# Order of the first steps and of the gathers and gates between attention and experts, in an attention-to-experts kernel on one Trainium2 core

## The chip, the cores and the metric

The kernel runs on one core of one Trainium2 chip, so there is no other core to exchange data with. The core has five engines that run side by side, each with its own instruction stream, and wait for one another by semaphores: TensorE (PE, matrix products and transposes), VectorE (DVE), ScalarE (ACT), GpSimd (POOL) and SyncE (SP, which here only issues transfers). Data lies in SBUF; matrix products land in PSUM; transfers between the device's memory and SBUF are done by 16 DMA engines. The metric is the device time of one execution in microseconds (us), as the median over runs. Beside the timed runs there is one execution with the hardware profiler, from which the page and every start time below come; it took 531.48 us, of which 529.5 lie between the first and the last instruction.

## The reference

The input is q, k, v of shape (4, 8, 768, 64) in float32: four batches, eight heads, 768 positions. Stage one is attention with a Λ-shaped mask and a linear bias per head; stage two sends each of the 3072 resulting tokens to one of eight experts.

```python
scores = scale * np.matmul(q, k.transpose(0, 1, 3, 2))
is_global = pos[None, :] < int(n_global)            # the first 8 positions
is_local = (rel >= 0) & (rel < int(n_local))        # the last 96 positions
keep = is_global | is_local
dist = np.where(is_global & ~is_local, float(n_local), np.abs(rel))
scores = np.where(keep, scores - slopes * dist, -1e9)
a = softmax(scores)
x = (a @ v).transpose(0, 2, 1, 3).reshape(3072, 512)

logits = x @ w_gate                                 # 8 experts
expert_idx = np.argmax(logits, axis=1)
gate_w = softmax(logits)[arange, expert_idx]
for e in range(8):                                  # tokens of expert e
    y[e] = np.maximum(x[e] @ w1[e], 0.0) @ w2[e]    # 512 -> 1024 -> 512
return gate_w[:, None] * y
```

## The kernel before

**Attention (to 161 us).** Positions are cut into six blocks of 128. A query block sees its own and the previous key block and the eight global keys. Heads go in pairs, two heads of 64 side by side in 128 partitions; 4 batches times 4 pairs give 16 pairs, in the code `pr`. A pair is worked in three units of two blocks each, so there are 48 units, `units[n]`. For a unit, `scores(n)` makes the products of Q with K (L507), ACT takes the exponential (L513, tile `e`), and DVE multiplies by the bias weights `Wb` (L520 for a pair's first unit, L524 for the others). `attend(n)` multiplies by V (L542, tile `o`), two units behind the scores; `turn(n)` transposes the attention's results (L559, tile `px`, copied at L561) for the router.

The keys come in two forms. `kT` holds K transposed. `kA` is a shifted copy, in which the first 8 columns of each block are replaced by the eight global keys; `keys_at` makes it with two ACT copies (L426 for the rest of the block, L428 for the global ones). Likewise `va` is V with the global rows in it (`turn_v`, ACT copies L452 and L453). `Wb` for a pair of heads is made by `weights(j)` with two ACT exponentials (L486) of the distances `distb`, which `bias()` builds on DVE (L477 to L482).

From the second pair on, K and Q come in strips by SP's transfers (L409) and DVE transposes them (`turn_qk`, L461 and L462). The first pair is different: its K and Q are loaded whole (`load_first`, blocks 0 to 2 first, then 2 to 6) and turned by PE against an identity matrix (`turn_first`, L442), as a first lot of two blocks before the scores of unit 0 and a second lot of four blocks after them. A lot's K is copied out of PSUM by DVE (L443), its Q by ACT (L444), then ACT makes `kA`. `weights(0)` is called ahead of unit 0's scores.

**Between attention and experts (161 to 197 us).** Each finished batch is routed: `logits`, `spread`, `tables` and `spread_sum` count the tokens of each expert and give each its place. Expert 0's first 256 tokens are worked early, in 16 small pieces of PE work (`early_hidden`, L347, and `early_result`, L354), which `work(n)` takes off a list `fill`, so that PE has something to do while DVE, ACT and POOL do the routing of the last batch. `fetch_0(i)` gathers these tokens from the device's memory by POOL's indirect transfers into `xq_0`; `take(1)` gathers those of the next expert, its `xq_0` and `xq_s` pieces, back to back (L284), and the early outputs `y_0_0` and `y_0_1` are written out after that. `xq_0` and `xq_s` are filled with zeros once (L211 and L774), so that the rows that no token fills are defined. `gates_of` (L273 to L280) multiplies the gate weights into a sparse form `mg` on DVE, sums them by a product (`pg`, L279, a tile of the pool `ps_m`) and copies the result out on DVE (L280); it is called twice in a row, between two calls of `work`.

**Experts (from 197 us).** The eight experts follow in order of size, with capacities of 464 tokens down to 272; expert 0 has 208 left after its early 256. `hidden(p)` makes the 1024 hidden values in eight steps (L1065), each followed by ACT's relu (L1067); `result(p)` or `along_row` makes the 512 outputs (L1102 or L1119). `pace(n, after)` issues up to n waiting gathers on POOL behind a given instruction, so that they are spread over an expert's work. `sort` transposes gathered tokens on DVE (L295).

What sets the order: the engines' streams are written out by hand under a manual schedule, so every engine runs its instructions as the Python code issues them; the pools' buffer counts and the semaphores that the framework derives set the waits. `tc.add_manual_dep`, in `behind`, adds a wait on a named instruction.

Of the kernel before, what the change touches and what calls it, by code (L numbers as in the profile page):

```python
# [16 lines left out]
P = 128  # L17
# [12 lines left out]
def kernel(  # L30
# [76 lines left out]

    ones_in(vts[0])

# [5 lines left out]
    iota_c = consts.tile([P, 1], F32)  # L115
    iota(iota_c, [[0, 1]], 0, 1)

    warm = consts.tile([P, 1], F32)
    nc.vector.memset(warm, 0.0)
    nc.scalar.activation(warm, warm, AF.Exp)  # L120
    load_first(2, NB)
    ident = consts.tile([P, P], F32)
    make_identity(nc, ident)
    rank_e = consts.tile([P, E], F32)
# [147 lines left out]

    def gates_of(pool, ps, nm, ns, gs, to):  # L273

        mg = pool.tile([P, NS, TB], F32, tag="mw", name="mg" + nm, bufs=1)[:, 0:ns, :]
        nc.vector.tensor_tensor(out=mg, in0=gs.rearrange("p (s o) -> p s o", o=1).to_broadcast([P, ns, TB]),
                                in1=grp.rearrange("p (o g) -> p o g", o=1).to_broadcast([P, ns, TB]), op=ALU.mult)
        pg = ps.tile([P, NS * TB], F32, tag="m", name="pg" + nm)[:, 0:TB * ns]
        nc.tensor.matmul(pg, lhsT=sel, rhs=mg.rearrange("p s g -> p (s g)"), start=True, stop=True)  # L279
        nc.vector.tensor_copy(out=to, in_=pg)  # L280

# [17 lines left out]
    def plan(p):  # L299
        if p < E:  # L300
            r = ORDER[p] - 2
            xqs[p] = xq_s[p % 2]
            cols = rows_0[1][:, 2 * TB:] if p == 1 else rows_s[:, NQ * TB * r:NQ * TB * r + NQ * TB]
            for i in range(pieces_of(CAPS[ORDER[p]])):
                pending.append((xqs[p], cols, i))

# [9 lines left out]
    def take(p):  # L316
        plan(p)
        while pending:
            gather_one(*pending.pop(0))

# [21 lines left out]
    def hidden_0(ph, q, f0, nf):  # L342

        for f in range(nf):
            c0 = P * (f0 + f)
            for kc in range(KC):
                nc.tensor.matmul(ph[:, P * f:P * f + P], lhsT=w1_0[:, 0, kc, c0:c0 + P], rhs=xe_0[:, kc, P * q:P * q + P],  # L347
                                 start=(kc == 0), stop=(kc == KC - 1))
        nc.scalar.activation(hT_0[q][:, f0:f0 + nf, :], ph.rearrange("p (f s) -> p f s", f=nf), AF.Relu)

    def result_0(po, q, f0, nf, later=None):

        for fc in range(f0, f0 + nf):
            nc.tensor.matmul(po, lhsT=hT_0[q][:, fc, :], rhs=w2_0[:, 0, fc, :],  # L354
                             start=(fc == 0), stop=(fc == FC - 1))
        if f0 + nf == FC:
            scaled(f"y_0_{q}", P, po, gslot_0[0][:, q:q + 1], idx_0[0][:, q:q + 1], later)

    def distances(dist, kpos, loc):
# [16 lines left out]
    def banded_attention():  # L376
        with ExitStack() as actx:
# [46 lines left out]

            def keys_at(kT, kA, a0, a1):
                nc.scalar.copy(out=kA[:, a0:a1, GW:P],  # L426
                                      in_=kT[:, a0 * P:a1 * P].rearrange("p (c t) -> p c t", t=P)[:, :, GW:P])
                nc.scalar.copy(out=kA[:, a0:a1, 0:GW],  # L428
                                      in_=kT[:, 0:GW].rearrange("p (o t) -> p o t", o=1).to_broadcast([P, a1 - a0, GW]))

# [4 lines left out]

            def turn_first(c0, c1, pt):

                qT, kT, kA = pairs[0][0:3]
                w = P * (c1 - c0)
                for i, t in enumerate((k_first, q_first)):  # L440
                    for c in range(c0, c1):
                        nc.tensor.transpose(pt[:, i, P * (c - c0):P * (c - c0) + P], t[:, c, :, :].rearrange("p h d -> p (h d)"), ident)  # L442
                nc.vector.tensor_copy(out=kT[:, P * c0:P * c1], in_=pt[:, 0, 0:w])  # L443
                nc.scalar.copy(out=qT[:, P * c0:P * c1], in_=pt[:, 1, 0:w])  # L444
                keys_at(kT, kA, max(c0 - 1, 0), c1 - 1)

# [45 lines left out]
            def blocks(c):  # L492

                return [(0, True), (1, False), (1, True)] if c == 0 else [(0, False), (0, True), (1, False), (1, True)]

            def scores(n):
                b, j, c = units[n]
                qT, kT, kA = pairs[b * NJ + j][0:3]
                bl = blocks(c)
                w = P * len(bl)  # L500
                ps = ps_s.tile([P, 2, 512], F32, tag="s", name=f"s_{n}")
                for m, (t, own) in enumerate(bl):
                    i = 2 * c + t
                    for h in range(2):
                        r = slice(D * h, D * h + D)
                        lhsT = kT[r, P * i:P * i + P] if own else kA[r, i - 1, :]
                        nc.tensor.matmul(ps[:, h, P * m:P * m + P], lhsT=lhsT, rhs=qT[r, P * i:P * i + P],  # L507
                                         start=True, stop=True)
# [4 lines left out]
                nc.scalar.activation(e[:, :, 0:w], ps[:, :, 0:w], AF.Exp, scale=D ** -0.5)  # L513
                if n == 0:
                    turn_first(2, NB, ps_s.tile([P, 2, 512], F32, tag="s", name="first_1"))
                    turn_v(0)
                elif c == 1 and b == 0 and j + 1 < NJ:
                    weights(j + 1)
                if c == 0:
                    nc.vector.tensor_tensor(out=e[:, :, 0:w], in0=e[:, :, 0:w], in1=W[:, 2 * j:2 * j + 2, 0:w],  # L520
                                            op=ALU.mult)
                else:
                    eh = e.rearrange("p h (t c) -> p h t c", t=2)
                    nc.vector.tensor_tensor(  # L524
                        out=eh, in0=eh,
                        in1=W[:, 2 * j:2 * j + 2, P:3 * P].rearrange("p h (o c) -> p h o c", o=1).to_broadcast([P, 2, 2, 2 * P]),
                        op=ALU.mult)
                st[n] = e
# [134 lines left out]
            def early_hidden(z, f0):  # L663
                ph = ps_s.tile([P, 2, 512], F32, tag="s", name=f"ph_0_{z}_{f0}")
                hidden_0(ph[:, 0, 0:2 * P], z, f0, 2)

            def early_result(z, f0):
                if f0 == 0:
                    st["po"] = ps_o.tile([P, DM], F32, tag="o", name=f"po_0_{z}")
                result_0(st["po"], z, f0, 2, later)  # L670

# [72 lines left out]
            pair_tiles(0)  # L744
            turn_first(0, 2, ps_o.tile([P, 2, 2 * P], F32, tag="o", name="first_0"))
            bias()
            weights(0)
            nu = len(units)
# [5 lines left out]
            for n0 in range(0, nu, 2):  # L754
# [5 lines left out]
                for n in two:  # L760
# [238 lines left out]
    with tc.manual_schedule():  # L999
        banded_attention()  # L1000

        take(1)
        while later:
            later.pop(0)()


        r2 = recips.rearrange("p a b -> p (a b)")
# [15 lines left out]
        with ExitStack() as ectx:  # L1023
# [31 lines left out]
            def hidden(p, between=None):  # L1055
# [6 lines left out]
                for fc in range(FC):  # L1062
# [23 lines left out]
            def along_row(p, C, w2t, hT):  # L1086
# [127 lines left out]
```

## Time and profile before

| what | value |
| --- | --- |
| time, median of 3 runs | 519.71 us (519.63 to 520.02) |
| span of the profiled execution | 529.5 us |
| PE's first record, and its first scores | 4.67 us, 6.68 us |
| PE's first early piece of expert 0 after the last unit's product with V | 161.32 us |
| PE's first record of expert 0's rest | 196.97 us |
| PE's last record | 520.1 us |

The page of the profile gives, for each engine, the time in which it was busy; then the span in 40 slices of 13.2 us, where a digit is the busy share of a slice in tenths; then the transfers, and groups of instructions with the idle time ahead of them and what ended it. Tiles carry their names from the program, but where SBUF is used again under another name the trace shows the older one: `w_second` stands for several buffers of the attention stage. In a timeline a row is `start, duration, engine, line, operation, out<-in, shape, count`, with the idle time before it in brackets and what ended that. PE's rows overlap, since matrix products are pipelined; the distance of two starts is what one costs.

### The profile page before, as it was taken

Reading aid. Unit: us, or ns where it says so; the run is one execution under the profiler, and the core shown is the slowest. Engines: PE = TensorE matmul, PEld = TensorE weight load, DVE = VectorE, ACT = ScalarE, POOL = GpSimd, SP = SyncE. Lnnn points to the kernel's source line nnn. Section 1 sums busy time; section 2 is a strip of 40 time slices with the busy share of each in tenths; the row PEclk is TensorE's granted clock in tenths of the full one; section 3 lists DMA queues with packets and bytes.
Section 4 is the critical chain, followed back from the end, with each engine's and each line's share of the span. In section 5 each row is a group of like instructions: output and inputs, shape, how many; then the busy total and the mean of one; then the engine's idle time right before and its main releaser. Section 6 shows DMA issues by size and latency. Waiting matters only on the chain.

```text
span 529.5 us, 7971 instructions
## 1 busy us (share of the span) xinstructions
PE 503.4 (95%) x3108; PEld 348.2 (66%) x3108; DVE 181.3 (34%) x484; ACT 126.7 (24%) x227; POOL 138.5 (26%) x161
## 2 busy tenths in 40 slices
PE   4999999999999995999999999999999999999992
PEld 3989999999999744975455445545545846545540
DVE  5867897896975423010120030021011011020010
ACT  4766655654642100101001101100100201101100
POOL 5000000000042474243344145325114625310010
PEclk9999999999999998999999999999999999999997
DMA  9899999999919712490825456173372685110000
GB/s 152 149 166 162 236 171 163 232 182 168 315 49 248 230 46 65 100 277 27 182 71 190 100 130 202 42 171 104 130 153 86 198 188 190 39 41 17 1 35 27
DMA packets 145184, 71.95 MB, mean 136 GB/s; under 512 B 126672, under 2 KB 126678, under 8 KB 145136
## 3 DMA queue, kind: packets, MB, share of 16 engines
q1 hardware_dynamic: 137344, 58.16, 48.3%
q0 software_dynamic: 5264, 12.59, 7.8%
q10 hardware_dynamic: 2528, 0.59, 0.6%
q8 instruction: 26, 0.43, 0.4%
q14 instruction: 22, 0.18, 0.1%
HBM read 59.00 MB, written 12.75 MB: 135 GB/s over the span
## 4 chain that ended last, share of the span: by engine, by line
PE 82%; another core or an unknown queue 5%; SPq 5%; DVE 3%; DMA 2%; ACT 1%; issue 1%; POOL 0%; POOLq 0%; ACTq 0%; DVEq 0%
PE ph L1065 29%; PE po L1119 26%; PE o L542 11%; PE s L507 5%; SPq L409 4%; PE ph L347 2%; PE po L1102 2%; PE px L559 2%; PE pt L1128 1%; PE pq L573 1%; PE pi L632 1%; DMA vt<-in_v_dram 1%; DMA x_tok<-xr 1%; DMA k_first<-in_k_dram 1%
## 5 line engine op out<-in xcount | busy, mean ns | idle before, releaser
L1067 ACT ACTIVATE hT<-ph 128x416 f32<-128x416 f32 (+4 forms) x64 | 29.6, 467 | 289.2 <-PE ph L1065 179.1
L284 POOL DMA_INDIRECT xq_s<-x_tok,rows_s x72 | 72.6, 1009 | 67.9 <-ACT hT L1067 39.2
L1065 PE MATMUL ph<-xe,w_first 128*128 128x208 f32 (+3 forms) x256 | 79.3, 471 | 6.2 <-ACT hT L1067 4.5
L335 DVE TENSOR_SCALAR y<-po,gslot_s 128x512 f32<-128x512 f32 (+1 forms) x17 | 12.8, 751 | 201.5 <-PE po L1119 201.5
L1065 PE MATMUL ph<-xe,w_second 128*128 128x416 f32 (+3 forms) x256 | 79.4, 470 | 0.0
L1119 PE MATMUL po<-w_second,hT 128*128 128x512 f32 (+1 forms) x176 | 76.2, 592 | 0.0
L1065 PEld LDWEIGHTS ph<-xe,w_first 128*128 128x128 f32 x256 | 50.2, 200 | 34.4 <-issue 11.4
L1065 PEld LDWEIGHTS ph<-xe,w_second 128*128 128x128 f32 x256 | 48.3, 190 | 29.3 <-issue 10.4
L1119 PE MATMUL po<-w_first,hT 128*128 128x512 f32 (+1 forms) x144 | 62.3, 592 | 0.0
L1119 PEld LDWEIGHTS po<-w_second,hT 128*128 128x128 f32 (+1 forms) x176 | 33.2, 189 | 41.3 <-issue 40.7
L284 POOL DMA_INDIRECT xq<-x_tok,rows x15 | 16.0, 1068 | 162.1 <-DVE rows L271 143.4
L542 PE MATMUL o<-vt,e 128*128 128x128 f32 x288 | 53.2, 275 | 0.0
L327 POOL DMA_INDIRECT out_dram<-y,idx_s x17 | 17.2, 1011 | 124.7 <-DVE xe L295 71.7
L1119 PEld LDWEIGHTS po<-w_first,hT 128*128 128x128 f32 (+1 forms) x144 | 27.2, 189 | 34.0 <-issue 33.5
L542 PE MATMUL o<-va,e 128*128 128x128 f32 x240 | 46.6, 276 | 0.1
L542 PEld LDWEIGHTS o<-vt,e 128*128 128x128 f32 x288 | 42.4, 192 | 0.1
L507 PE MATMUL s<-qT,kT 64*128 64x128 f32 x384 | 38.6, 285 | 0.9 <-ACT qT L444 0.9
L513 ACT ACTIVATE e<-s 128x1024 f32<-128x1024 f32 (+1 forms) x36 | 33.2, 945 | 26.1 <-PE s L507 26.1
L507 PE MATMUL s<-qT,kA 64*128 64x128 f32 x320 | 34.3, 292 | 3.2 <-ACT kA L428 3.2
L542 PEld LDWEIGHTS o<-va,e 128*128 128x128 f32 x240 | 36.4, 192 | 0.4 <-issue 0.3
L507 PEld LDWEIGHTS s<-qT,kT 64*128 64x128 f32 x384 | 30.2, 196 | 2.2 <-ACT qT L444 1.3
L524 DVE TENSOR_TENSOR e<-e,Wb 128x1024 f32<-128x1024 f32 x24 | 28.7, 1210 | 7.6 <-ACT e L513 7.3
(189 smaller groups left out, 502.8 us busy)
## 6 DMA issues: line engine op xcount, KB each, us to landing
w_second<-in_moe_w_dram SPq DMA_DIRECT2D x16, 512.0 KB, 9.0
w_second<-in_moe_w_dram SPq DMA_DIRECT2D x4, 2048.0 KB
x_tok<-xr SPq DMA_DIRECT2D x24, 256.0 KB, 3.6
w_first<-in_moe_w_dram SPq DMA_DIRECT2D x12, 512.0 KB, 7.7
w_first<-in_moe_w_dram SPq DMA_DIRECT2D x3, 2048.0 KB
vt<-in_v_dram SPq DMA_DIRECT2D x31, 192.0 KB, 3.8
w_second<-in_q_dram SPq DMA_DIRECT2D x60, 96.0 KB, 3.3
w_second<-in_k_dram SPq DMA_DIRECT2D x60, 96.0 KB, 2.8
```

What stands on the lines that cost most here:

```text
L284: return nc.gpsimd.indirect_dma_start(out=xq[:, i, :], out_offset=None, in_=x_tok[0:NJ * top, :], in_offset=bass.IndirectOffsetOnAxis(ap=c ...
L327: p = nc.gpsimd.indirect_dma_start(out=to[:, :], out_offset=bass.IndirectOffsetOnAxis(ap=where, axis=0), in_=y[0:rows, :], in_offset=None, ...
L335: done = nc.vector.tensor_scalar(out=y[0:rows, :], in0=po[0:rows, :], scalar1=gs[0:rows, :], scalar2=None, op0=ALU.mult)
L347: nc.tensor.matmul(ph[:, P * f:P * f + P], lhsT=w1_0[:, 0, kc, c0:c0 + P], rhs=xe_0[:, kc, P * q:P * q + P], start=(kc == 0), stop=(kc == ...
L409: nc.sync.dma_start(t[p0:p0 + 32, :, :], src[b, 2 * j + h].rearrange("(c t) d -> t c d", t=32)[:, :, 32 * d:32 * d + 32])
L507: nc.tensor.matmul(ps[:, h, P * m:P * m + P], lhsT=lhsT, rhs=qT[r, P * i:P * i + P], start=True, stop=True)
L513: nc.scalar.activation(e[:, :, 0:w], ps[:, :, 0:w], AF.Exp, scale=D ** -0.5)
L524: nc.vector.tensor_tensor(out=eh, in0=eh, in1=W[:, 2 * j:2 * j + 2, P:3 * P].rearrange("p h (o c) -> p h o c", o=1).to_broadcast([P, 2, 2, ...
L542: nc.tensor.matmul(po[:, t, h, :], lhsT=pt[:, h, P * m:P * m + P], rhs=(vt if own else va)[:, c0:c0 + P], start=(m == mine[0][0]), stop=(m ...
L1065: nc.tensor.matmul(ph[:, 0:C], lhsT=w1t[:, 0, kc, P * fc:P * fc + P], rhs=xe[:, kc, 0:C], start=(kc == 0), stop=(kc == KC - 1))
L1067: done = nc.scalar.activation(hT[:, fc, 0:C], ph[:, 0:C], AF.Relu)
L1119: nc.tensor.matmul(po[0:rows, :], lhsT=hT[:, fc, P * q:P * q + rows], rhs=w2t[:, 0, fc, :], start=(fc == 0), stop=(fc == FC - 1))
```

## The change

The change has two halves. They have in common that work which isn't needed yet is taken out of the way of work that is.

At the start: POOL makes the identity matrix first and some constants later; the second half of the first pair's loads is issued on ACT before ACT loads its exponential table; the first pair is turned in three lots of two blocks, one before the scores of unit 0 and two behind them, with K and Q in separate PSUM tiles; the first pair's `kA` is copied by DVE in place of ACT; `weights(0)` is called after the second lot in place of ahead of unit 0; the zero fills of `xq_0` and `xq_s` wait for the exponentials of units 18, 24, 30 and 36.

At the passage to the experts: the gathers of expert 0's rest go through the list of waiting gathers, two at once and the others one for each piece of `work`, and those of the next expert follow on the same list, one for each piece and one for each step of `hidden(0)`; `take(1)` is gone. The early outputs are put, and the gathered tokens of the next expert sorted, between the steps of `along_row`. `gates_of` is cut in two: `mg` is made ahead of `hidden(0)`, the products and copies come behind it, in the experts' pool of PSUM tiles. The three pieces of `work` around the gates become one call.

```diff
-    ones_in(vts[0])
+    ident = consts.tile([P, P], F32)
+    make_identity(nc, ident)
...
+    ones_in(vts[0])
+    load_first(2, NB)
     warm = consts.tile([P, 1], F32)
     nc.vector.memset(warm, 0.0)
     nc.scalar.activation(warm, warm, AF.Exp)
-    load_first(2, NB)
-    ident = consts.tile([P, P], F32)
-    make_identity(nc, ident)
...
-    for t in xq_0:
-        nc.gpsimd.memset(t, 0.0)
...
-            def keys_at(kT, kA, a0, a1):
-                nc.scalar.copy(out=kA[:, a0:a1, GW:P], ...)
-                nc.scalar.copy(out=kA[:, a0:a1, 0:GW], ...)
+            def keys_at(kT, kA, a0, a1, copy=nc.scalar.copy):
+                copy(out=kA[:, a0:a1, GW:P], ...)
+                copy(out=kA[:, a0:a1, 0:GW], ...)
...
-            def turn_first(c0, c1, pt):
+            def turn_first(c0, c1):
+                pk = ps_o.tile([P, 2 * P], F32, tag="o", name=f"first_k{c0}")
+                pq = ps_m.tile([P, 2 * P], F32, tag="m", name=f"first_q{c0}")
...
-                keys_at(kT, kA, max(c0 - 1, 0), c1 - 1)
+                keys_at(kT, kA, max(c0 - 1, 0), c1 - 1, nc.vector.tensor_copy)
...
                 if n == 0:
-                    turn_first(2, NB, ps_s.tile([P, 2, 512], F32, tag="s", name="first_1"))
+                    turn_first(2, 4)
+                    weights(0)
+                    turn_first(4, NB)
                     turn_v(0)
...
             bias()
-            weights(0)
...
-                    if n == nu // 2 or n == nu // 2 + 2:
-                        nc.gpsimd.memset(xq_s[(n - nu // 2) // 2], 0.0)
+                    if n % 6 == 0 and n // 6 in (3, 4, 5, 6):
+                        behind(nc.gpsimd.memset((xq_0 + xq_s)[n // 6 - 3], 0.0), exps[n], ...)
```

```diff
             def fetch_0(i):
-                    gather(xq_0[h], rows_0[i][:, TB * h:TB * h + TB], min(n, TB), N - S if i == 0 else N)
+                    for k in range(min(n, TB)):
+                        pending.append((xq_0[h], rows_0[i][:, TB * h:TB * h + TB], k, N - S if i == 0 else N))
+                if i == 0:
+                    while pending:
+                        gather_one(*pending.pop(0))
+                else:
+                    for _ in range(2):
+                        gather_one(*pending.pop(0))
+                    plan(1)
...
             def work(pieces):
-                    do(z, f0)
+                    pace(1, do(z, f0))
...
-            work(1)
-            gates_of(gp, ps_m, "_s", NR * NQ, gslot_s.rearrange("p r q -> p (r q)"), gpc_s)
-            gates_of(gp, ps_m, "_1", LOTS[1], gslot_0[1], gpc_0)
             fit()
-            work(2)
+            work(3)
...
-        take(1)
-        while later:
-            later.pop(0)()
...
-                    pace(1 if fc < FC - 1 else len(pending), done)
+                    pace(1 if fc < FC - 1 or p == 0 else len(pending), done)
...
+                    if 0 < dc < KC - 1:
+                        sort(1, dc - 1, KC - 2)
+                        later.pop(0)()
...
-            sort(1, 0, 1)
+            spread_gates = [gates_of(hp, "_s", ..., gpc_s), gates_of(hp, "_1", ..., gpc_0)]
             hidden(0)
+            for do in spread_gates:
+                do(ps_t)
```

More of the change, by code (lines that the diff above doesn't have):

```diff
@@ L271, in rows_of, with gates_of, rest @@
         nc.vector.tensor_scalar(out=to_rows, in0=pw, scalar1=float(NJ), scalar2=j_of[:, 0:1], op0=ALU.mult, op1=ALU.add)
-    def gates_of(pool, ps, nm, ns, gs, to):
-        mg = pool.tile([P, NS, TB], F32, tag="mw", name="mg" + nm, bufs=1)[:, 0:ns, :]
+    def gates_of(pool, nm, ns, gs, to):
+        mg = pool.tile([P, ns, TB], F32, tag="mg" + nm, name="mg" + nm, bufs=1)
         nc.vector.tensor_tensor(out=mg, in0=gs.rearrange("p (s o) -> p s o", o=1).to_broadcast([P, ns, TB]),
                                 in1=grp.rearrange("p (o g) -> p o g", o=1).to_broadcast([P, ns, TB]), op=ALU.mult)
-        pg = ps.tile([P, NS * TB], F32, tag="m", name="pg" + nm)[:, 0:TB * ns]
-        nc.tensor.matmul(pg, lhsT=sel, rhs=mg.rearrange("p s g -> p (s g)"), start=True, stop=True)
-        nc.vector.tensor_copy(out=to, in_=pg)
+        def rest(ps):
+            pg = ps.tile([P, DM], F32, tag="pt", name="pg" + nm)[:, 0:TB * ns]
+            nc.tensor.matmul(pg, lhsT=sel, rhs=mg.rearrange("p s g -> p (s g)"), start=True, stop=True)
+            nc.vector.tensor_copy(out=to, in_=pg)
+        return rest
     def gather_one(xq, cols, i, top=N):
@@ L304, in plan @@
             for i in range(pieces_of(CAPS[ORDER[p]])):
-                pending.append((xqs[p], cols, i))
+                pending.append((xqs[p], cols, i, N))
     def behind(inst, after, reason):
@@ L314, in pace @@
             behind(gather_one(*pending.pop(0)), after, "spreads the gathers over the experts' work")
[L316 to L319, printed above, removed]
     scatters = []
@@ L346, in hidden_0 @@
             for kc in range(KC):
-                nc.tensor.matmul(ph[:, P * f:P * f + P], lhsT=w1_0[:, 0, kc, c0:c0 + P], rhs=xe_0[:, kc, P * q:P * q + P],
-                                 start=(kc == 0), stop=(kc == KC - 1))
+                done = nc.tensor.matmul(ph[:, P * f:P * f + P], lhsT=w1_0[:, 0, kc, c0:c0 + P],
+                                        rhs=xe_0[:, kc, P * q:P * q + P], start=(kc == 0), stop=(kc == KC - 1))
         nc.scalar.activation(hT_0[q][:, f0:f0 + nf, :], ph.rearrange("p (f s) -> p f s", f=nf), AF.Relu)
+        return done
     def result_0(po, q, f0, nf, later=None):
         for fc in range(f0, f0 + nf):
-            nc.tensor.matmul(po, lhsT=hT_0[q][:, fc, :], rhs=w2_0[:, 0, fc, :],
-                             start=(fc == 0), stop=(fc == FC - 1))
+            done = nc.tensor.matmul(po, lhsT=hT_0[q][:, fc, :], rhs=w2_0[:, 0, fc, :],
+                                    start=(fc == 0), stop=(fc == FC - 1))
         if f0 + nf == FC:
             scaled(f"y_0_{q}", P, po, gslot_0[0][:, q:q + 1], idx_0[0][:, q:q + 1], later)
+        return done
     def distances(dist, kpos, loc):
@@ L423, in banded_attention @@
             pairs = {}
-            def keys_at(kT, kA, a0, a1):
[L426 to L429, printed above, removed]
+            def keys_at(kT, kA, a0, a1, copy=nc.scalar.copy):
+                copy(out=kA[:, a0:a1, GW:P], in_=kT[:, a0 * P:a1 * P].rearrange("p (c t) -> p c t", t=P)[:, :, GW:P])
+                copy(out=kA[:, a0:a1, 0:GW],
+                     in_=kT[:, 0:GW].rearrange("p (o t) -> p o t", o=1).to_broadcast([P, a1 - a0, GW]))
             def pair_tiles(pr):
@@ L434, in pair_tiles @@
                 return pairs[pr]
-            def turn_first(c0, c1, pt):
+            def turn_first(c0, c1):
                 qT, kT, kA = pairs[0][0:3]
                 w = P * (c1 - c0)
-                for i, t in enumerate((k_first, q_first)):
+                pk = ps_o.tile([P, 2 * P], F32, tag="o", name=f"first_k{c0}")
+                pq = ps_m.tile([P, 2 * P], F32, tag="m", name=f"first_q{c0}")
+                for pt, t in ((pk, k_first), (pq, q_first)):
                     for c in range(c0, c1):
-                        nc.tensor.transpose(pt[:, i, P * (c - c0):P * (c - c0) + P], t[:, c, :, :].rearrange("p h d -> p (h d)"), ident)
-                nc.vector.tensor_copy(out=kT[:, P * c0:P * c1], in_=pt[:, 0, 0:w])
-                nc.scalar.copy(out=qT[:, P * c0:P * c1], in_=pt[:, 1, 0:w])
-                keys_at(kT, kA, max(c0 - 1, 0), c1 - 1)
+                        nc.tensor.transpose(pt[:, P * (c - c0):P * (c - c0) + P], t[:, c, :, :].rearrange("p h d -> p (h d)"), ident)
+                nc.vector.tensor_copy(out=kT[:, P * c0:P * c1], in_=pk[:, 0:w])
+                nc.scalar.copy(out=qT[:, P * c0:P * c1], in_=pq[:, 0:w])
+                keys_at(kT, kA, max(c0 - 1, 0), c1 - 1, nc.vector.tensor_copy)
             def turn_v(pr):
@@ L494, in blocks @@
                 return [(0, True), (1, False), (1, True)] if c == 0 else [(0, False), (0, True), (1, False), (1, True)]
+            exps = {}
             def scores(n):
@@ L512, in scores @@
                     e = ep.tile([P, 2, 512], F32, tag="e", name=f"e_{n}")
-                nc.scalar.activation(e[:, :, 0:w], ps[:, :, 0:w], AF.Exp, scale=D ** -0.5)
+                exps[n] = nc.scalar.activation(e[:, :, 0:w], ps[:, :, 0:w], AF.Exp, scale=D ** -0.5)
                 if n == 0:
-                    turn_first(2, NB, ps_s.tile([P, 2, 512], F32, tag="s", name="first_1"))
+                    turn_first(2, 4)
+                    weights(0)
+                    turn_first(4, NB)
                     turn_v(0)
@@ L664, in early_hidden @@
                 ph = ps_s.tile([P, 2, 512], F32, tag="s", name=f"ph_0_{z}_{f0}")
-                hidden_0(ph[:, 0, 0:2 * P], z, f0, 2)
+                return hidden_0(ph[:, 0, 0:2 * P], z, f0, 2)
             def early_result(z, f0):
@@ L669, in early_result @@
                     st["po"] = ps_o.tile([P, DM], F32, tag="o", name=f"po_0_{z}")
-                result_0(st["po"], z, f0, 2, later)
+                return result_0(st["po"], z, f0, 2, later)
             for do in (early_hidden, early_result):
@@ L744, in banded_attention @@
             pair_tiles(0)
-            turn_first(0, 2, ps_o.tile([P, 2, 2 * P], F32, tag="o", name="first_0"))
+            turn_first(0, 2)
             bias()
-            weights(0)
             nu = len(units)
@@ L772, in banded_attention @@
                         weights_0.pop(0)()
-                    if n == nu // 2 or n == nu // 2 + 2:
-                        nc.gpsimd.memset(xq_s[(n - nu // 2) // 2], 0.0)
+                    if n % 6 == 0 and n // 6 in (3, 4, 5, 6):
+                        behind(nc.gpsimd.memset((xq_0 + xq_s)[n // 6 - 3], 0.0), exps[n], "fills wait until the start is over")
                 if n0 >= 4:
@@ L1132 @@
             ground()
-            sort(1, 0, 1)
+            spread_gates = [gates_of(hp, "_s", NR * NQ, gslot_s.rearrange("p r q -> p (r q)"), gpc_s),
+                            gates_of(hp, "_1", LOTS[1], gslot_0[1], gpc_0)]
             hidden(0)
+            for do in spread_gates:
+                do(ps_t)
             fetch(2, 0)
```

## The prediction

> **What bounds the kernel now.** I read the page first, then the list of what TensorE (PE) waited for up to 215 us, then each engine's timeline around those waits. The page: busy time per engine, then the busy tenths of forty slices of 13.2 us each.
>
> ```profile
> PE 503.4 (95%) x3108; PEld 348.2 (66%) x3108; DVE 181.3 (34%) x484; ACT 126.7 (24%) x227; POOL 138.5 (26%) x161
> ...
> PE   4999999999999995999999999999999999999992
> ...
> DMA  9899999999919712490825456173372685110000
> ```
>
> PE is the bound: only the first slice, the one at about 200 us and the last are not full. So an edit earns only what it takes out of PE's idle time, and the list of waits (total, times, longest) says how much there is:
>
> ```profile
> PE ph L1065 <- ACT hT L1067: 4.5, 1, 4.5
> PE s L507 <- ACT kA L428: 3.2, 2, 2.0
> ...
> PE pg L279 <- DVE gpc_s L280: 1.4, 1, 1.4
> PE s L507 <- ACT qT L444: 0.9, 1, 0.9
> ```
>
> The diff touches the last three directly, the first perhaps. At the start PE turns K and Q of blocks 2 to 5 (from 8.26; the four records at 9.17 take 1.06), then waits for ScalarE's (ACT) copies of shifted keys. PE's timeline (start, duration, idle time before in brackets):
>
> ```profile
> 12.23 0.80 PE L507 MATMUL s<-qT,kA 64*128 64x128 f32 x4 [2.01 <-ACT kA L428]
> ```
>
> ACT's timeline before it: two bias exponentials (Wb), then, in the lines left out, the first scores' exponential (10.05), qT (10.98) and the long key copy (11.47), then the short one:
>
> ```profile
> 9.21 0.94 ACT L486 ACTIVATE Wb<-distb 128x384 f32<-128x384 f32 x2 [2.29 <-DVE distb L482]
> ...
> 11.93 0.24 ACT L428 COPY kA<-kT 128x64 f32<-128x64 f32 x1
> ```
>
> **What the Trainium skill says.** "SBUF — State Buffer", section "Who interferes with whom": copies, casts and TENSOR_SCALAR on VectorE (DVE) can take a port pair that they share with GpSimd (POOL), and are then held until a GpSimd operation is over; a DVE instruction with two SBUF inputs isn't held by a GpSimd operation that only writes. The trace agrees: the 128x256 TENSOR_SCALAR at 6.50 took 1.69 us and ended as the fills of xq_s did (two of 2.91 together from 5.14, so at about 8.1); the 128x256 TENSOR_TENSOR behind it took 0.42. "TensorE: Matmul & The Clock Gate", section "Part 1: The HAM clock gate (the "warmup" mystery)": PE's clock is halved until PE has been busy for some microseconds. The trace agrees: matmuls of the first units start 0.21 us apart until about 15.6, and 0.11 after.
>
> **The change, part by part.**
>
> (a) Start: the first loads are issued earlier on ACT, pair 0 is turned in three lots in PSUM tiles of their own, its shifted keys go to DVE, Wb comes after the second lot's qT, the fills go later. Taken from ACT ahead of unit 1's scores: the two Wb (10.05 - 9.21 = .84) and both kA copies (.57 + .24). DVE gets two copies per lot, and with the fills gone its 1.69 should be .42, so the distances end 1.3 us sooner. Timeline that I expect: scores(0) end at about 8.1, as K's landing sets them; the second lot has two blocks, four transposes at .27 (1.06 / 4), done by 9.2; then kT .42 (the 128x256 copy at 5.79) and kA about .3 + .2 on DVE beside qT .37 on ACT. Unit 1's scores start at 9.6 to 10.2 instead of 12.23: 2.0 to 2.6 us.
>
> How much of it stays? Two later points hold what follows. First, DVE's timeline, where pair 1's keys come by DMA (the line left out is qT's turn at 15.34, .94):
>
> ```profile
> 14.44 0.98 DVE L461 STREAM_TRANSPOSE kT<-w_second 128x768 f32<-128x768 f32 x1 [2.61 <-DMA w_second<-in_k_dram]
> ...
> 16.20 1.18 DVE L524 TENSOR_TENSOR e<-e,Wb 128x1024 f32<-128x1024 f32 x1
> ```
>
> These stand ahead of unit 1's weighting, which ends at 17.38; PE's product o_1 begins at 18.21, .8 later. So at o_1 only .8 of the 2.6 is left. Second, ACT waits for the V of a later pair from the same transfer stream, and what follows runs without a gap up to the key copy at 34.04:
>
> ```profile
> 29.28 0.74 ACT L452 COPY va<-vt 128x650 f32<-128x650 f32 x1 [3.92 <-DMA vt<-in_v_dram]
> ...
> 34.04 0.25 ACT L428 COPY kA<-kT 128x80 f32<-128x80 f32 x1
> ```
>
> PE's scores of unit 9 start at 34.34, after 1.15 us of waiting for that copy. The order on ACT from 29.28 to 34.04 is the same in the new kernel. However early PE is before, it comes back at 34.3 while that V lands at 29.2. So the start earns 0, or up to the .8 left at o_1 if the stream is as much faster (ACT's Q load of the first blocks, issued at 3.67 in the old kernel, no longer stands behind its table load). I take 0.3.
>
> (b) What that order costs: the sync queue's loads now wait for landings that come .3 to .8 later (n_local at 3.4 to 3.65, then Q), so its first load of pair 1 goes at about 4.8 instead of 4.0. The skill, "DMA: Bandwidth & Descriptors", section "Queues, rings and completion order": the sync and ACT queues are rings on the same 16 DMA engines, which take packets from them in turn. So what matters is whether the engines idle; the DMA row is at 9 in nearly every slice to 158 us, the second at 8, which agrees. Bounds: 0 if no byte is lost, .8 if the whole delay arrives at 29.2. I take 0.2.
>
> (c) Fills of xq_0 (two of 1.01) and xq_s (two of 2.91) behind the exponentials of units 18, 24, 30, 36, some 65, 86, 108 and 130 us. POOL has time. PE's closest waits for DVE in the attention have .04 to .3 us of slack by semaphore times (turned x at 71, 109, 147). Bounds: 0, as most of DVE's work there is TENSOR_TENSOR or comes from PSUM, and about 2 us, if a copy like that at 6.50 is held by each long fill in a tight place. I take 0.1.
>
> (d) Gates. PE where the attention ends:
>
> ```profile
> 184.49 0.46 PE L279 MATMUL pg_s<-mg_s,sel 128*128 128x96 f32 x2
> 186.34 0.40 PE L279 MATMUL pg<-mg,sel 128*128 128x24 f32 x2 [1.39 <-DVE gpc_s L280]
> ```
>
> Both products use one PSUM tile, so PE waits until DVE has copied pg_s out (185.94 to 186.20). From 184.95, where pg_s ends, PE idles 1.4; before it .1 to .3 for mg_s: up to 1.8. Of this 1.0 is DVE's gap from pg_s's end to its copy's start (185.94 - 184.95), which may be lateness of the profile's own signals. Moved behind expert 0's hidden layer, the products cost .46 + .40 as they do here, DVE's copies lie beside the down projection, and the fill pieces run on. Gain .9 to 1.8; I take 1.3.
>
> (e) Gathers of experts 1 and 2, 1.0 us each on POOL (the page's indirect groups: 1,009 and 1,068 ns): one per piece of work instead of back to back from 186. The last, behind expert 0's hidden layer, lands some 3.5 us later, and the transposes (seven in 1.46 at 193.71) end about 1 us before PE wants them by my count. Those of expert 0 itself keep some 5 us. I take 0; being late would cost at most the 1.46. The puts of the early outputs go later on POOL, where nobody waits for them.
>
> Sum: -1.3 - 0.3 + 0.2 + 0.1 = -1.3, and 519.71 - 1.3 = **518.4**.
>
> **Rivals.** *Given back* (.22): V lands later by (b)'s middle, .4 to .8, the start earns nothing, the gates .9 or less: 519.4 to 519.7. For: the 3.92 at 29.28. Against: the gates need no transfer. *Start in full* (.11): in the timed executions V comes early enough, and 1.2 to 2.5 us more stay: 516. For: landing times vary. Against: 3.92 is a long wait to vanish. *The stall at 203 us is real* (.07). ACT and PE there:
>
> ```profile
> 207.35 0.81 ACT L1067 ACTIVATE hT<-ph 128x208 f32<-128x208 f32 x3 [26.07 <-remote]
> 207.75 7.51 PE L1065 MATMUL ph<-xe,w_first 128*128 128x208 f32 x25 [4.53 <-ACT hT L1067]
> ```
>
> PE has its PSUM full from 203 and comes back at half clock (.25 a record until 213.6, .175 after): 6.5 + 3 = 9.5 us. It falls at the end of the burst of gathers of 186 to 203, which (e) spreads; then 510. Against: the profiled execution took 531.48, 11.8 more than the timed ones, and PE shows no other room for that, so I hold the stall for the profiled execution's alone. *Slower* (.10): DVE held at the fills and V later, with a late last gather: 519.7 + 1.2 = 520.9.
>
> **How the numbers follow.** The main case has .50, from 517.5 to 519.2. The range, 515.5 to 520.4, takes in the start in full and the gain given back; outside lie the stall, most of slower and the tails, under .2. Faster by over 0.2% is below 518.67: about .35 of the main case, .11 and .07, so .53. Slower is above 520.75: .10 and a tail of the others, .12. The rest, .35, is the same.
>
> **What would show it.** Unit 1's scores at 9.6 to 10.2 with no 2.0 wait for kA; o_1 at about 17.4; ACT's V copy still at 29.3 after a longer wait, and unit 9 at 34.3 within .5; no PE wait for gpc_s. I am wrong if unit 9 moves by over 1 us either way, if PE waits for a DVE copy by the fills, if it waits for expert 1's tokens, or if the stall of 203 goes and the timed median falls by 9.

## The result, and the profile after

The changed kernel took 523.77 us (median of 4, 522.95 to 524.39) against 519.73 for the kernel before: a ratio of 1.0076, with an interval from 1.0058 to 1.0093, so 4 us slower where 1.3 us less had been forecast. On one chip of the later runs the kernel before took 531.83 us (13 runs, 529.61 to 533.75), and 521.7 to 522.1 on three others, so every comparison below is with the kernel before on the same chip.

The page of the changed kernel, busy times and busy tenths as before (slices of 13.1 us):

```profile
PE 500.5 (96%) x3108; PEld 345.7 (66%) x3108; DVE 180.7 (35%) x491; ACT 126.7 (24%) x224; POOL 138.7 (27%) x161
...
PE   5889999999996999999999999999999999999993
...
DMA  8999998999927911781833546275182586000001
```

The hole of the kernel before, in the sixteenth slice, is gone, and another one stands in the thirteenth. PE's list of waits names it:

```profile
PE pq L577 <- DVE early L671: 4.6, 1, 4.6
PE s L509 <- DVE qT L462: 1.8, 1, 1.8
PE s L509 <- ACT kA L426: 1.5, 1, 1.5
```

`pq` is the product of the last batch's router, and `early` is a small comparison on DVE. Nothing about either was changed. PE's timeline there, first in the kernel before (start, duration), then in the changed kernel:

```profile
163.72 1.95 PE L347 MATMUL ph<-xe,w_first 128*128 128x128 f32 x16
165.60 1.51 PE L573 MATMUL pq<-w_second,wg_sb 128*32 128x192 f32 x32
167.04 2.05 PE L347 MATMUL ph<-xe,w_first 128*128 128x128 f32 x16
```

```profile
163.72 1.95 PE L344 MATMUL ph<-xe,w_first 128*128 128x128 f32 x16
170.29 2.79 PE L577 MATMUL pq<-w_second,wg_sb 128*32 128x192 f32 x32 [4.62 <-DVE early L671]
173.01 2.05 PE L344 MATMUL ph<-xe,w_first 128*128 128x128 f32 x16
```

Both kernels are at the same point at 163.72. The changed one loses 4.69 us up to the start of `pq`, and 1.28 more in `pq` itself, which runs at about half rate behind the pause (2.72 from its start to the start of the next product, against 1.44): 5.97 in all. DVE tells why it is late; this is the changed kernel, the transposes of expert 0's early tokens:

```profile
164.52 0.31 DVE L297 STREAM_TRANSPOSE xe<-xq 128x128 f32<-128x128 f32 x1 [0.60 <-DMA xq<-x_tok,rows]
169.88 0.31 DVE L297 STREAM_TRANSPOSE xe<-xq 128x128 f32<-128x128 f32 x1 [5.05 <-DMA xq<-x_tok,rows]
170.12 0.12 DVE L671 TENSOR_SCALAR early<-c 128x1 f32<-128x1 f32 x1
```

The eighth and last of the first gathers lands at about 169.9. DVE works in the order of its program, so `early` waits behind its transpose, and PE behind `early`. The two kernels differ in what GpSimd and the sync queue did shortly before. Kernel before, GpSimd's first and last early gather, then the 2 MB load of the next expert's first weights (the row's name `w_second` is the buffer's):

```profile
151.44 1.21 POOL L284 DMA_INDIRECT xq<-x_tok,rows  x1 [143.38 <-DVE rows L271]
...
161.62 1.00 POOL L284 DMA_INDIRECT xq<-x_tok,rows  x1 [0.30 <-issue]
```

```profile
163.44 1.96 SPq L256 DMA_DIRECT2D w_second<-in_moe_w_dram  x4
```

The same in the changed kernel:

```profile
152.38 1.21 POOL L286 DMA_INDIRECT xq<-x_tok,rows  x1 [29.41 <-DVE recips L550]
...
162.74 1.00 POOL L286 DMA_INDIRECT xq<-x_tok,rows  x1 [0.30 <-issue]
```

```profile
163.05 2.36 SPq L254 DMA_DIRECT2D w_second<-in_moe_w_dram  x4
```

The weight load followed the start of the last gather after 1.82 us, and now follows it after 0.31: the gather starts 1.12 later, and the load leaves 0.39 sooner. The gather had landed by 164.40 in the kernel before, 2.8 us after its start, and takes 7.1 us in the changed one. **The theory** that I took from this: the weight load overtakes the last gather in the DMA engines, because the gathers start about 1 us later. This is called the race below; it is lost where PE then waits for `early`. Rivals: the gather is late by itself; the spread gathers or the changed start do it.

At the gates the change did what it should (changed kernel, PE: the products now lie behind expert 0's hidden layer, with no wait):

```profile
188.45 12.21 PE L352 MATMUL po<-w_first,hT 128*128 128x512 f32 x28
200.50 11.42 PE L1068 MATMUL ph<-xe,w_first 128*128 128x208 f32 x64
211.75 0.36 PE L279 MATMUL pg_s<-mg_s,sel 128*128 128x96 f32 x2
211.94 0.33 PE L279 MATMUL pg<-mg,sel 128*128 128x24 f32 x2
212.11 11.50 PE L1105 MATMUL po<-hT,w_first 128*128 128x208 f32 x64
```

### The profile page after: what moved, and what is told of

Same layout as the page of the kernel before. It is cut to its first block, busy times and chain, and to the rows that moved or that the text cites. A ratio compares the mean times of both kernels' runs of the same rounds, so it can differ in the third digit from the quotient of the medians.

```text
span 522.5 us, 7997 instructions
## 1 busy us (share of the span) xinstructions
PE 500.5 (96%) x3108; PEld 345.7 (66%) x3108; DVE 180.7 (35%) x491; ACT 126.7 (24%) x224; POOL 138.7 (27%) x161
## 4 chain that ended last, share of the span: by engine, by line
PE 87%; DMA 3%; DVE 3%; issue 2%; SPq 1%; POOL 1%; ACT 1%; POOLq 0%; ACTq 0%; DVEq 0%
PE ph L1068 30%; PE po L1125 26%; PE o L546 12%; PE s L509 7%; PE po L352 3%; PE px L563 2%; PE po L1105 2%; PE ph L344 2%; PE pt L1134 1%; PE pq L577 1%; DMA xq<-x_tok,rows 1%; SPq L408 1%; POOL xq L286 1%; DMA vt<-in_v_dram 1%; PE pi L636 1%
## 5 line engine op out<-in xcount | busy, mean ns | idle before, releaser
L1068 PE MATMUL ph<-xe,w_first 128*128 128x208 f32 (+3 forms) x256 | 75.8, 457 | 0.1
L1068 PEld LDWEIGHTS ph<-xe,w_first 128*128 128x128 f32 x256 | 47.5, 190 | 27.6 <-issue 10.7
```

The lines of the kernel that those rows point to most:

```text
L1068: nc.tensor.matmul(ph[:, 0:C], lhsT=w1t[:, 0, kc, P * fc:P * fc + P], rhs=xe[:, kc, 0:C], start=(kc == 0), stop=(kc == KC - 1))
```

## The experiments

The kernels ran on four chips. All compute the whole of the reference. The kernel before ran beside them: 531.83 us on the first chip, 521.87 on the second, 522.08 on the third, 521.71 on the fourth.

**First chip: hold the load, delay the gathers, old fills, second half alone**

*e1: the changed kernel with a wait on the weight load.*

```diff
-            expert_w1(w1_1, slice(1, 2))
+            behind(expert_w1(w1_1, slice(1, 2))[0], turned, "weights wait for the last gather")
```

Here `turned` is the transpose of the last early gather.

> The changed kernel with one wait added: the 2 MB load of the next expert's first weights waits on the sync queue until the last of expert 0's first eight gathers has been turned on VectorE. Theory (the weight load overtakes the last gather): the profile shows no wait of over 0.5 us of TensorE at 165 to 171 us, the last gather lands within 3.5 us of its start (7.1 in the changed kernel), and the time falls by the 4.6 us of waiting and some 1.3 us of half clock, to 517.5 to 518.5. Rival (the last gather is late by itself, as it starts 1.1 us later): the wait stays at over 3 us and the time at 523 to 524.

*e2: the kernel before, with GpSimd held up ahead of the first gathers.*

```diff
+                if i == 0:
+                    late = gp.tile([P, 512], F32, tag="late", name="late", bufs=1)
+                    nc.gpsimd.tensor_copy(out=late[:, 0:1], in_=rows_0[0][:, 0:1])
+                    nc.gpsimd.memset(late, 0.0)
```

> The kernel before with a copy of one column and a fill of 128x512 on GpSimd ahead of expert 0's first gathers, about 1.2 us, so that these start when those of the changed kernel do; nothing else. Theory (a race of the last gather with the weight load, which is lost by about 1 us of delay): TensorE waits 4 to 5 us at 165 to 171 us and the time rises by 5 to 7 us, to 525 to 527. Rival (the cause is in the changed start or in the spread gathers): the delay is hidden or passed on as it is, 519.7 to 521.

*e3: the changed kernel with the fills where they were.*

```diff
-                    if n % 6 == 0 and n // 6 in (3, 4, 5, 6):
-                        behind(nc.gpsimd.memset((xq_0 + xq_s)[n // 6 - 3], 0.0), exps[n], ...)
+                    if n == nu // 2 or n == nu // 2 + 2:
+                        nc.gpsimd.memset(xq_s[(n - nu // 2) // 2], 0.0)
...
+    for t in xq_0:
+        nc.gpsimd.memset(t, 0.0)
```

> The changed kernel with the four zero fills back at the start, as in the kernel before. Theory: the first gather starts 0.3 us after its row numbers, as before, in place of 0.9, so the last starts some 0.6 us sooner, at about 162.1; whether it then wins the race isn't known beforehand: either 517.5 to 519 with no wait, or 523 to 524 with the same 4 to 5 us. Rival (the fills delay VectorE in the middle of the attention): TensorE's times at 149 us fall by more than 0.3 us, and the time by as much and no more.

*e4: the kernel before with the second half of the change (the second block of the change's diff above) and nothing of the first.*

> The kernel before with only the second half of the change: spread gathers, gates behind expert 0's hidden layer, later outputs. Start and fills as before. Theory (the gates earn, the gathers of the start of this passage keep their times and win the race): no wait of TensorE at 165 to 171 us, expert 0's hidden layer starts 2.4 us sooner than in the kernel before, and the time is 517.2 to 518.2. Rival (the spread itself costs, by late tokens or by instructions in GpSimd's way): 520 or more, with waits of TensorE after 186 us.

Measured: e1 521.12, e2 534.22, e3 521.10, e4 521.48, with the kernel before at 531.83 (ratios 0.980, 1.0055, 0.979, 0.979). All four miss the times that the theory expected. None of them shows the wait for `early`. But the comparison is swamped by something else: the kernel before is 10 us slower here. The profile of e2, which has the kernel before's burst of gathers, shows on ACT and PE what the profile of the kernel before showed at 203 us:

```profile
210.75 0.82 ACT L1071 ACTIVATE hT<-ph 128x208 f32<-128x208 f32 x3 [26.20 <-remote]
```

```profile
211.15 8.78 PE L1069 MATMUL ph<-xe,w_first 128*128 128x208 f32 x40 [4.79 <-ACT hT L1071]
```

e4 spreads the gathers, has no such line, and is 10.35 us below the kernel before on this chip. The kernel before itself has no profile here, but its time and e2's profile say that the stall, which I had put down to the profiled execution, is in the timed runs of this chip, and that it goes with the second half of the change. In e2 it also upset the test: DVE and ACT waited for PE's signals to 165.88 and 166.04, and the weight load, which comes behind the stores of the last tokens, left only at 167.39, when the gathers had landed (the last four are transposed from 166.44 on). As to the race, e1 to e4 decide nothing, since the changed kernel itself, with the loss, wasn't run on this chip.

**Second chip: the changed kernel again, and the second half in two parts**

*e5* is the changed kernel. *e6* is the kernel before with the gates alone moved:

```diff
-            work(1)
-            gates_of(gp, ps_m, "_s", ...)
-            gates_of(gp, ps_m, "_1", ...)
             fit()
-            work(2)
+            work(3)
...
             sort(1, 0, 1)
+            spread_gates = [gates_of(hp, "_s", ...), gates_of(hp, "_1", ...)]
             hidden(0)
+            for do in spread_gates:
+                do(ps_t)
```

*e7* is e4 without these lines: only the gathers are spread, and the outputs put later.

> The changed kernel as it is, side by side with the kernel before and with the parts below. In the first session the kernel before took 519.7 and the changed one 523.8; on the chip of the last runs the kernel before took 531.8. Theory (the kernel before has a stall of some 10 us behind its burst of gathers at 186 to 203 us on this chip and hadn't in the first session's timed runs; the changed one has none): the changed kernel is at 520 to 525 here while the kernel before is at 530 to 533, if it is such a chip. Rival (this chip is slower for everything): the changed kernel is some 4 us over the kernel before here too, about 535.

> The kernel before with the gates part alone: products and copies of the gates behind expert 0's hidden layer. The gathers stay in one burst. Theory (the burst makes the stall): TensorE still waits 4 us and more at 200 to 212 us, and the time is the kernel before's less 1.5 to 2.5. Rival (the gates' back-to-back products with their copies cause it): no wait there and 520 to 522.

> The kernel before with the gathers of experts 1 and 2 spread, one for each piece of work and each step of expert 0's hidden layer, and the later outputs; the gates stay where they were. Theory (the burst makes the stall): no wait of over 1 us at 200 to 212 us, and the time is 2 to 2.5 over that of the whole second half, 523 to 524, as the wait for the gates' copy stays. Rival (gates cause it): 529 to 532 with the wait.

Measured: e5 525.01, a ratio of 1.0055 (1.0036 to 1.0073), so 3.1 over, with a wait of 3.6 for `early`. e6 521.06, 0.9982 (0.9972 to 0.9992), so 0.8 below. e7 521.33, 0.9984 (0.9975 to 0.9992), so 0.5 below. The stall isn't there in either, also not with the burst kept, so the pair didn't tell which of the two takes it away on the first chip. Both times miss: e6 gains less than the 1.5 to 2.5 expected, and e7, expected at 523 to 524, gains as well. e7 shows the gates' wait without late signals: PE idles 0.44 ahead of `pg`, not 1.39, and what it waits for last is `mg`, which DVE makes behind the copy of `pg_s`:

```profile
185.59 0.40 PE L279 MATMUL pg<-mg,sel 128*128 128x24 f32 x2 [0.44 <-DVE mg L276]
```

e7 also shows a wait of 1.3 us for expert 1's tokens at 220 us, which e6, with the burst kept, hasn't.

**Third chip: hold and delay again, the start alone, and a mended kernel**

*e8* has e1's edit and *e9* has e2's. *e10* is the kernel before with the first half of the change, but with the old fills. *e11* is the changed kernel with e1's wait, e3's fills, and

```diff
-                    pace(1, do(z, f0))
+                    pace(2 if f0 % 4 == 0 else 1, do(z, f0))
```

> The changed kernel with the next expert's weight load held until the last of expert 0's first eight gathers is turned, again, for a chip on which the kernel before has no stall at 200 us (520 to 522). Theory (overtaking makes the loss): 4 to 5 us less than the changed kernel has over the kernel before on such chips (3.1 and 4.0 over), so 0.5 to 2 us below the kernel before, with no wait for the product of the router at 163 to 171 us. Rival (the loss has another source too): within 0.5 us of the kernel before or above it.

> The kernel before with about 1.2 us of other work on GpSimd ahead of the first gathers, again, for such a chip. Theory: the weight load follows the last gather by 0.2 to 0.4 us where it was 1.4 to 1.9, the gather lands 6 to 7 us after its start, TensorE waits 3.5 to 5 us for it and the time is 4.5 to 6 us over the kernel before. Rival (a late gather alone does nothing): 0 to 1.2 us over. On a chip where the kernel before stalls at 200 us the run tells nothing of this.

> The kernel before with the first half of the change alone: order of the first loads and constants, pair 0 in three lots, shifted keys on VectorE, bias exponentials later; the zero fills stay where the kernel before has them. Theory (the lead of 2.4 us at unit 1 is given back at the V load of the third pair and at pair 1's keys): scores of unit 9 within 0.5 us of the kernel before's, counted from the landing of the first keys, and a time within 0.7 us of the kernel before. Rival (the lead stays): 1.5 to 2.5 us below.

> The changed kernel with three things mended: the weight load held behind the last early gather, the zero fills at the start as in the kernel before, and gathers two at a time behind five of the pieces of work, so that the last of expert 1's are issued three steps of the hidden layer sooner. Expected: no wait at 163 to 171 us, no wait of over 0.3 us for expert 1's tokens at 220 us (0.4 to 2.0 in the runs with spread gathers), and 1 to 2.5 us below the kernel before where that has no stall, 11 to 13 below where it has. Rival (the later lots contend with the weights or lag on the chip that lags): no better than the hold alone.

| kernel | us | ratio to the kernel before (522.08) |
| --- | --- | --- |
| e8, changed with the load held | 519.11 | 0.9948 (0.9929 to 0.9968) |
| e9, before with delayed gathers | 527.48 | 1.0106 (1.0082 to 1.0129) |
| e10, before with the new start | 520.71 | 0.9974 (0.9964 to 0.9984) |
| e11, all mended | 518.04 | 0.9922 (0.9904 to 0.9941) |

e9 shows the loss from the other side: in the kernel before, about 1 us of other work on GpSimd is enough to make it. GpSimd's last early gather, the sync queue's weight load, and DVE's transpose of that gather:

```profile
162.87 1.00 POOL L284 DMA_INDIRECT xq<-x_tok,rows  x1 [0.30 <-issue]
```

```profile
163.00 1.99 SPq L256 DMA_DIRECT2D w_second<-in_moe_w_dram  x4
```

```profile
169.40 0.31 DVE L295 STREAM_TRANSPOSE xe<-xq 128x128 f32<-128x128 f32 x1 [4.51 <-DMA xq<-x_tok,rows]
```

The load follows after 0.13, the gather takes 6.5, PE waits 4.1, and the time is 5.4 over, as expected. In e8 the gathers start as late as in the changed kernel, at 162.60 for the last, but the load waits until 166.16. The gather then takes 3.2 us, and PE's wait is what is left of that:

```profile
PE pq L578 <- DVE early L672: 0.7, 1, 0.7
```

So the late start of the gathers by itself costs 0.7 us; the load close behind costs the rest. e8 is 3.0 below the kernel before, more than the 0.5 to 2 expected, so its rival, another source of loss, falls.

"Overtakes" says a little too much. The trace also keeps the single packets: the last gather is 16 packets of 4096 bytes on GpSimd's queue, and the load's packets have that size on the sync queue. In the eleven executions where the load was held or followed after 1.4 us or more, its first packet starts after the gather's last. In the five where it followed after 0.1 to 0.3 us (the changed kernel, e5, e9, e13, e14), 5 to 16 of the gather's packets start after the load's first. In e13 below, the gather's start from 164.45 to 167.16 and the load's from 165.35 on; in e12, the gather's from 163.30 to 163.74 and the load's from 164.54 on. So the packets of the two mix, and the transpose has to wait for the gather's last.

e10 is 1.4 below the kernel before (0.8 to 1.9 by its interval), over the 0.7 that I allowed. The interval reaches into the 1.5 to 2.5 of a lead that stays; that it doesn't stay is seen in the trace, best against e9, which has the old start. V, then PE's unit 9, in e9:

```profile
29.57 0.74 ACT L452 COPY va<-vt 128x650 f32<-128x650 f32 x1 [3.16 <-DMA vt<-in_v_dram]
```

```profile
34.63 0.49 PE L507 MATMUL s<-qT,kA 64*128 64x128 f32 x4
```

and in e10:

```profile
29.00 0.74 ACT L453 COPY va<-vt 128x650 f32<-128x650 f32 x1 [4.26 <-DMA vt<-in_v_dram]
```

```profile
34.06 0.49 PE L508 MATMUL s<-qT,kA 64*128 64x128 f32 x4 [1.38 <-ACT kA L427]
```

Unit 1 starts at 11.24 in e10 and at 14.80 in e9, 3.6 us sooner. At unit 9 there is 0.57 left, which is just what the copy of V starts sooner by; 2.2 of the other 3 us are PE's waits in e10 for qT (0.84, at 16.58) and for this copy (1.38).

e11 is 4.0 below, more than the 1 to 2.5 expected, and has neither wait.

**Fourth chip: which edit makes the gathers late**

*e12* is e3 again. *e13* is the kernel before with the late fills alone, the reverse of e3's edit. *e14* is the changed kernel.

> The changed kernel with the four zero fills back at the start, again, for a chip where the kernel before is at 520 to 522. Theory (the late fills make the gathers late): first gather 0.3 us after its row numbers, weight load 1.4 to 1.9 us after the last gather, no wait at 165 to 171 us, and 1 to 3.5 us below the kernel before. Rival (the changed start does it): the wait of 3 to 5 us stays and the time is 3 to 4 over.

> The kernel before with the late zero fills alone. Theory (they are enough): weight load under 1 us after the last gather, which lands 6 us or more after its start, TensorE waits 3.5 us or more, and the time is 4.5 to 7 us over the kernel before. Rival (they need the shift of the changed start as well): gathers 0.6 to 0.9 us later, but the race is won, and the time is within 1 us.

> The changed kernel as it is, beside the two others. Both theories: 3 to 4 us over the kernel before where that is at 520 to 522, with the wait at 165 to 171 us; if the kernel before is at 530 or more on this chip, some 6 to 10 below it.

| kernel | us | ratio to the kernel before (521.71) | last gather, load behind it |
| --- | --- | --- | --- |
| e12, changed with the old fills | 518.82 | 0.9946 (0.9926 to 0.9965) | 161.28, 1.46 |
| e13, before with the late fills | 526.75 | 1.0104 (1.0078 to 1.0131) | 162.65, 0.32 |
| e14, changed | 524.33 | 1.0049 (1.0035 to 1.0064) | 162.71, 0.31 |

The late fills are enough by themselves, and without them the changed kernel gains; so neither the changed start nor the spread gathers are needed for the loss. In e13 the fills delay the gathers in two places. GpSimd in e13 (row numbers done at 151.22 + .22 on DVE):

```profile
121.34 1.49 POOL L774 MEMSET xq_s<- 128x1664 f32 x1 [17.00 <-ACT e L513]
152.33 1.20 POOL L282 DMA_INDIRECT xq<-x_tok,rows  x1 [29.50 <-DVE recips L546]
153.84 1.01 POOL L282 DMA_INDIRECT xq<-x_tok,rows  x1 [0.31 <-issue]
155.15 2.00 POOL L282 DMA_INDIRECT xq<-x_tok,rows  x1 [0.30 <-issue]
```

and in e12 (row numbers done at 150.99 + .22):

```profile
151.50 1.20 POOL L288 DMA_INDIRECT xq<-x_tok,rows  x1 [143.46 <-DVE rows L271]
153.01 1.01 POOL L288 DMA_INDIRECT xq<-x_tok,rows  x1 [0.31 <-issue]
154.32 1.45 POOL L288 DMA_INDIRECT xq<-x_tok,rows  x1 [0.30 <-issue]
```

The fill itself is long over, at 122.8. But with late fills the first gather waits for one thing more, the fill. In the compiled program of e13, as in that of the changed kernel, the gather then carries the wait for the fill itself, and the wait for the row numbers stands in an instruction ahead of it; in that of e12 the gather carries the wait for the row numbers. From row numbers to gather it takes 0.89 us in place of 0.29. The third gather takes 2.00 in place of 1.45; why wasn't tried. 0.6 and 0.55 make 1.15, which is the way from 1.46 in e12 to 0.32 in e13. In e13 the gather lands 5.8 us after its start (the transpose begins at 168.47) and PE waits 3.3, both a little less than expected; e14 is 2.6 over, where 3 to 4 were expected.

## Why the prediction was wrong

**The fills (c)** are the step that failed. It said "POOL has time", bounded the cost by VectorE's held forms, and took 0.1. The VectorE side was right: in e13 PE has no wait between 40 and 150 us, where all four fills lie, and the TENSOR_TENSOR beside the last of them (121.91) isn't held (0.92 us, against a mean of 0.94 for its kind):

```profile
121.91 0.92 DVE L520 TENSOR_TENSOR e<-e,Wb 128x768 f32<-128x768 f32 x1
```

(The one at 8.23 that the prediction cites for this began when the fills were over, at 8.05, and shows nothing.) What (c) left out is that the gathers write the tiles that are filled, and so have to wait for the fills. A moved fill rearranges the waits of GpSimd's first gathers, thirty microseconds later, and behind them stand the transposes, `early` and PE. The fills measured +5.0 alone (e13), and 5.5 in the changed kernel (e14 less e12), where (c) had 0.1.

**The race** is in no step and no rival. Step (e) looked at the gathers of experts 1 and 2 and gave those of expert 0's rest 5 us of room; it never asked for the room of the first eight, nor what is sent on the other queue behind them. The trace of the kernel before had the numbers: last gather at 161.62, landed by 164.40, 2 MB of weights at 163.44. My "slower" rival named held DVE forms and a late last gather, but of expert 1, and 1.2 us in place of 4.

**Gates (d)**: right in direction, and in size just under the lower bound: 0.8 measured (e6, 0.4 to 1.5 by its interval), 0.9 to 1.8 forecast, 1.3 taken. The 1.0 of late signals, which I had half counted, is not there in e7, and PE waits there for `mg` too, not for the copy alone.

**Spread gathers (e)**: taken as 0, measured 0.5 below (e7, 0.4 to 1.3). The room for expert 1's tokens, 1 us by my count, isn't always there: PE waits at 220 us for 1.3 (e7), 2.0 (e3) and 0.4 (e1, e4), and not at all in the changed kernel, e5, e8, e12, e14 and e11, whose gathers go earlier.

**Start (a), (b)**: unit 1 at 9.86 where 9.6 to 10.2 was forecast, and the copy of V, not the lead at unit 1, decides unit 9 (34.65 in the changed kernel, V at 29.59, against 34.34 and 29.28). What ended that copy's wait was V's transfer in e10 and in e5, the changed kernel again; in the forecast comparison's own trace it is put down to PE. I took a gain of 0.1 net; e10 measured 1.4. Some 0.6 of it is V's earlier landing; where the rest comes from isn't settled, as single profiles of that stretch differ by that much. (b) reads the DMA row as at 9 to 158 us; its twelfth slice, from 146 us on, is at 1.

**The stall at 203 us** was a rival with .07, argued away with the timed runs. At 519.7 it had no room in the comparison that was forecast, as I held; but on the first chip it is in the timed runs too (531.83), and e4 without the burst is 10 us faster there. Its sum, 9.5, holds, though a record at half clock takes .35 and not .25. What makes PE's signals late on one chip isn't settled. Neither the changed kernel itself nor gates and spread apart were run on it.

The parts measured on chips without the stall, in us, with a minus for a gain: -0.8 (e6) - 0.5 (e7) - 1.4 (e10) + 5.0 (e13) = +2.3, against 2.6 to 4.0 measured for the changed kernel. With the loss taken away e12 is 2.9 below the kernel before, and e11 4.0, the best of all.

## What to carry to other kernels

When a filling or any other early instruction is moved, look at the next instruction in a hurry that uses the same tile: it can inherit a wait on the moved one, which costs even if that one is long over (0.6 us here). Where a small gather and a large prefetch leave on different queues close together (0.3 us apart was too close here, 1.4 us was enough, and nothing between was tried), write the order down as a dependency, as e1 does; an order that only the times give was lost here at a delay of 1 us. And take the waits from several executions before one is called an accident of the profile.

## What the runs showed of the hardware

A gather of 128 rows lands 2.7 to 3.2 us after its start with 2 MB of weights issued on another queue 1.4 us or more behind it, or held, and 5.8 to 7.1 us with the weights 0.1 to 0.3 us behind. Having been issued first didn't protect it: in those five executions 5 to 16 of its 16 packets start after the first packet of the weights.

A GpSimd gather that waits for its row numbers through an instruction ahead of it starts 0.88 to 0.89 us after them (six executions with late fills), and one that carries the wait itself 0.29 to 0.30 (eight with early ones).

The same program can have PE's signals arrive late on one chip and not on another. e2 and e9 are one program, at 534.22 and 527.48 us (e9 has the wait for `early` in it, e2 hasn't). In e2 PE's last early product is over by 201.98, where its next line starts, and DVE, which waited for it, goes on at 210.54. In e9 PE's next line starts at 201.52, and DVE goes on at 201.72:

```profile
210.54 0.75 DVE L335 TENSOR_SCALAR y<-po,gslot 128x512 f32<-128x512 f32 x1 [12.75 <-remote]
```

```profile
201.72 0.75 DVE L335 TENSOR_SCALAR y<-po,gslot 128x512 f32<-128x512 f32 x1 [4.74 <-PE po L354]
```
